# Spreading one-off loads over the steps of a pipelined stage, and putting a small copy first at that stage's start

## The chip, the cores and the metric

The kernel runs on one core of a Trainium2 chip. The metric is the device time of one execution, in microseconds (us), lower is better. The runs of one kernel in the same rounds lay within 0.15% (after, 4 runs) in one case and 1.4% (before, the 11 runs beside `start_only`) in another, and the same unaltered kernel gave medians between 1366 and 1376 us on the chips used here, so only runs of the same rounds on the same chip are compared with each other.

## The reference

The computation is the forward pass of a Branchformer-like block (attention in one branch, a gated depthwise convolution in the other, a depthwise merge convolution with K = 5 taps) and all its gradients. B = 2 sequences of T = 4000 tokens, D = 144 channels, bfloat16.

```python
# cut to what the change touches
m  = jnp.concatenate([glob, loc], axis=-1)            # two branches, 288 channels
mp = jnp.pad(m, ((0, 0), (pad, pad), (0, 0)))
mc = jnp.zeros_like(m)
for i in range(K):                                    # merge convolution, 5 taps
    mc = mc + mp[:, i:i + T, :] * dw_merge[i][None, None, :]
m = m + mc
return x + jnp.einsum('btc,cd->btd', m, w_merge)
# reference(): this and jax.vjp of it with grad_out -> out, dx, and 7 weight gradients
```

The gradients of the merge need the sum over all tokens of (output gradient, shifted by each tap) times (branch output). The kernel calls this the correlation and accumulates it in `EF`.

## The kernel before: the parts that matter

Each sequence goes through a head, an attention stage and a tail. The tail (`phase_tail`) runs in half steps h of two 128-token blocks each; a group g is four blocks, so h = 2g and 2g+1 belong to group g. For each group it

- loads `gs` (the output gradient with its five taps, 720 KB), `ug` (144 KB), `dh` (288 KB) and x (144 KB), the first three about two groups ahead, x at the group's start;
- correlates (`corr`) on TensorE. Its matmuls take 128 of the 144 channels, so the last 16 channels of each of the five taps are gathered into a narrow tile `g80` by GpSimd;
- writes 16 transposed rows to DRAM five times, each shifted by a tap (`taps.store`), and reads them back as 80 rows (`fill`), because the output convolution (`out_mm`) uses them as one operand `r80` a few half steps later.

```python
def prep(g):                                           # GpSimd, for group g
    r = slice(g * 4, g * 4 + 4)
    nc.gpsimd.memset(t3[:, r, 48:128], 0.0)
    nc.gpsimd.tensor_scalar(t3[:, r, 0:32], dh[:, r, 256:2 * D], 1.0, 0.0, ...)
    nc.gpsimd.tensor_scalar(t3[:, r, 32:48], S.Zn[:, r, 128:D], 1.0, 0.0, ...)
    g80 = G["g80", g] = lx.tile([128, 4, 80], BF, tag="g80", name="g80")
    nc.gpsimd.tensor_scalar(g80[:]..., G["gs", g][:, :, :, 128:D], 1.0, 0.0, ...)

# ... the main loop of the tail
loads(0); load_x(0); loads(1); prep(0)
for h in range(NPR + 4):                               # NPR = 16
    g, hf = divmod(h, 2)
    if hf == 0 and 0 < g < NGR:
        load_x(g)
    if 0 < h < NPR:
        turn_dx2(*turn_dx(h))                          # transposes of dh, Zn, t3
    if hf == 0 and g < NGR:
        turn(g, 0); corr(g, 0)                         # turn() ends with taps.store
        turn(g, 1); corr(g, 1)
    elif g < NGR:
        corr(g, 2)
        corr(g, 3)
    if h == 0:
        turn_dx2(*turn_dx(0))
    # ...
    if hf == 1 and 0 <= g - 1 < NGR:
        fill(g - 1)                                    # the two r80 loads
    # ...
    if h in (4, 6) and fin_:                           # second sequence only
        (fin_.loads if h == 4 else fin_.out_dwc)()
    # ...
    if 0 <= h - 4 < NPR:
        out_mm(h - 4)                                  # uses r80
    # ...
    if hf == 1 and g + 2 < NGR:
        loads(g + 2)                                   # gs, ug, dh
```

Every one of these transfers is issued by SyncE, in program order. An issue that must wait for something (an `r80` load must wait until the stores it reads from have landed; up to 4.5 us in the second tail of the kernel before) holds up all issues behind it.

`fin_.loads` exists only in the second sequence's tail. It fetches, in one piece of 11 issues at h = 4, what the final merge gradients need: the first sequence's `EF` sum in float32 (0.8 MB), its `gr` sum (288 KB) and eight weight tiles (0.8 MB together, one of them a few KB).

```python
def loads(self):
    for name, (dr, shp) in W.fin.items():              # WoT UT0 UT1 U0 U1 WmT Wqkv
        F[name] = fp.tile(shp, BF, name="f_" + name)
        nc.sync.dma_start(F[name][:], dr[:])
    # ...
    nc.sync.dma_start(self.EF0[:, 0:10, :], A.EF_d[:, 0:10, :])
    nc.sync.dma_start(self.EF0[0:80, 10:12, :], A.EF_d[0:80, 10:12, :])
    nc.sync.dma_start(self.gr0[:], A.gr_d[:])
    nc.sync.dma_start(self.Wk32[32:48, :], self.k.w_qkv[128:D, D:2 * D])
    # ... memsets
```

## Time and profile before

| | before |
|---|---|
| time, median of 3 runs | 1366.36 us (1363.06 to 1368.82) |
| profiled execution | span 1377.2 us, mean granted TensorE clock 0.977 |
| first tail, second tail: first to last correlation matmul | 72.6 us, 78.6 us |
| first use of r80 in half step 4 to that in half step 15, first and second tail | 51.2 us, 57.1 us |

The last two rows are worked out from matmul start times in the trace. I call them the *correlation stretch* and the *steady stretch*. The steady stretch leaves out the tail's start and its end; TensorE alone needs about 9.0 us for two half steps in it (in the first tail of before it is busy 49.5 of the 51.2 us of these 11 half steps).

The head of the profile's page (span, busy time of each engine, shares of the chain of work that ended last), kernel before:

```profile
span 1377.2 us, 40121 instructions
...
PE 1255.9 (91%) x15366; PEld 980.7 (71%) x15366; DVE 934.5 (68%) x3185; ACT 802.0 (58%) x2362; POOL 516.7 (38%) x919
...
PE 63%; DVE 12%; issue 8%; DMA 6%; ACT 5%; POOL 4%; SPq 1%; ACTq 0%; POOLq 0%; DVEq 0%
```

TensorE (PE) is busy 91% of the span and is 63% of the chain, so a wait of TensorE that goes away can be worth its length, and more where the granted clock was lower after it (0.50 after both waits shown below).

The waits of TensorE over the second tail and the end of the program, kernel before. The columns are what waited, what it waited for, the sum in us, how often, and the longest:

```profile
PE po L1992 <- DMA r<-y: 4.3, 1, 4.3
PE EF L1967 <- POOL g L1940: 3.0, 1, 3.0
PE pt L1977 <- POOL t3r L1938: 1.2, 1, 1.2
```

Two waits stand out. The first matters at the tail's start: the correlation waits 3.0 us for `g80`. The GpSimd timeline there (start, duration, line, operation, and in brackets the idle time before it with its cause) shows why:

```profile
1255.71 0.37 POOL L1936 MEMSET t3r<- 128x320 bf16 x1
1258.44 0.30 POOL L1937 TENSOR_SCALAR t3r<-dhr 128x128 bf16<-128x128 bf16 x1 [2.36 <-DMA dhr<-dh_d]
1258.71 0.24 POOL L1938 TENSOR_SCALAR t3r<-B_t 128x64 bf16<-128x64 bf16 x1
1258.91 0.46 POOL L1940 TENSOR_SCALAR g<-gs 128x320 bf16<-128x320 bf16 x1
```

The copy into `g80` (L1940) needs only `gs`, which is there, but it stands third in line behind a copy that waits 2.36 us for the DMA of `dh`. After the wait the microsecond windows show TensorE at clock 0.50 for 3.4 us, from about 1259.5 to 1262.9. The first tail shows the same (a wait of 3.05 us, then clock 0.50 from about 597.3 to 600.7).

The other wait, 4.3 us for `r80` (`r<-y`), lies in half step 6. The timeline of SyncE's DMA issues just before it, kernel before:

```profile
1277.62 0.45 SPq L1469 DMA_DIRECT2D y<-r  x1
1278.17 0.49 SPq L1469 DMA_DIRECT2D u<-r  x1
1278.71 0.42 SPq L2140 DMA_DIRECT2D f_WoT<-wf_WoT  x1
...
1284.00 0.43 SPq L2143 DMA_DIRECT2D f_EF<-EF_d  x1
...
1285.89 0.42 SPq L1472 DMA_DIRECT2D r<-y  x1
```

The 11 issues of `fin_.loads` begin at 1278.71 and end at 1285.85; the `r80` load stands behind all of them. One-microsecond windows of the same place (busy share and count for PE, weight loads, DVE, ACT, POOL, then the granted clock, the share of the DMA engines that was busy, GB/s):

```profile
1287.00:1288.00 1.00, 0.00 (x0) 0.00 (x0) 0.89 (x5) 0.02 (x1) 0.34 (x1) 1.00 0.95 348
...
1290.00:1291.00 1.00, 0.00 (x0) 0.00 (x0) 0.00 (x0) 0.00 (x0) 0.00 (x0) 0.60 1.20 216
1291.00:1292.00 1.00, 0.85 (x8) 0.85 (x9) 0.00 (x0) 0.00 (x0) 0.00 (x0) 0.50 1.04 321
...
1296.00:1297.00 1.00, 1.00 (x11) 1.00 (x9) 0.00 (x0) 0.97 (x4) 0.55 (x2) 0.50 0.00 0
```

TensorE stands still from 1286.8 to 1291.15, and after that runs at clock 0.50 until about 1297.

### The profile page before, as it was taken

The page shows a single profiled execution, that of the slowest core. Times are in us where ns is not written, and L with a number is a line of the kernel's source. Part 1 is how long each engine was busy: PE and PEld are TensorE (multiplying, and loading weights), DVE is VectorE, ACT ScalarE, POOL GpSimd, SP SyncE. Part 2 cuts the span into 40 slices and gives each one's busy share as a digit, 9 for nine tenths or more (in the row PEclk, how much of TensorE's full clock was granted, in tenths as well). Part 3 has the DMA queues.
Part 4 walks back from the last instruction along what each step waited for, and adds up shares of the span by engine and source line. Part 5 has one row for each costly group of instructions (what it writes and reads, how often), then busy time and mean ns, then how long its engine had stood idle before and what let it go on. Part 6 is the DMA issues. An engine that isn't in the chain of part 4 may idle for free.

```text
span 1377.2 us, 40121 instructions
## 1 busy us (share of the span) xinstructions
PE 1255.9 (91%) x15366; PEld 980.7 (71%) x15366; DVE 934.5 (68%) x3185; ACT 802.0 (58%) x2362; POOL 516.7 (38%) x919
## 2 busy tenths in 40 slices
PE   5799999999999998989878999999999999998896
PEld 2657777777776776789755777777776677668884
DVE  5466788688776785746454777877777677773564
ACT  3766666666666564444276666666665666543442
POOL 2212344444343342345340243444444344323550
PEclk9999999999999999999988999999999999999998
DMA  4459999999998989857563999999898889996761
GB/s 131 132 99 161 172 170 167 156 182 170 165 150 157 179 164 168 165 158 197 154 191 71 168 157 174 174 156 178 146 179 159 142 171 155 193 171 153 220 156 28
DMA packets 649706, 218.17 MB, mean 158 GB/s; under 512 B 587648, under 2 KB 646944, under 8 KB 649504
## 3 DMA queue, kind: packets, MB, share of 16 engines
q1 hardware_dynamic: 648448, 215.39, 80.7%
q8 instruction: 122, 2.00, 0.6%
q14 instruction: 80, 0.66, 0.1%
q10 hardware_dynamic: 1056, 0.13, 0.1%
HBM read 56.77 MB, written 23.89 MB: 59 GB/s over the span
## 4 chain that ended last, share of the span: by engine, by line
PE 63%; DVE 12%; issue 8%; DMA 6%; ACT 5%; POOL 4%; SPq 1%; ACTq 0%; POOLq 0%; DVEq 0%
PE y L1825 15%; PE pS L1786 8%; PE X L1845 7%; PE X L1846 7%; PE pD L1786 6%; PE pS L1782 4%; DVE Sm L1792 3%; PE pc L1518 2%; ACT Pm L1791 2%; DMA gnC<-gnC_d 2%; PE pb L1432 2%; PE po L1991 2%; PE EF L1967 1%; PE gr L2062 1%; POOL cc L2031 1%
## 5 line engine op out<-in xcount | busy, mean ns | idle before, releaser
L1792 DVE SCALAR_TENSOR_TENSOR Sm<-pD,Pm 128x500 bf16<-128x500 f32 x512 | 326.2, 674 | 210.2 <-ACT Pm L1791 191.5
L1791 ACT ACTIVATE Pm<-pS 128x500 bf16<-128x500 f32 x512 | 295.7, 585 | 91.2 <-PE pS L1786 87.2
L1845 PE MATMUL X<-Qs,Sm 128*128 128x144 bf16 x2048 | 292.9, 227 | 5.0 <-DVE acc L1858 5.0
L1846 PE MATMUL X<-Bt,Pm 128*128 128x144 bf16 x2048 | 293.0, 227 | 0.0
L1856 POOL TENSOR_TENSOR acc<-xs,acc 128x432 f32<-128x432 f32 x150 | 167.1, 1114 | 229.0 <-ACT xs L1855 228.6
L1846 PEld LDWEIGHTS <-Pm 128*128 128x128 bf16 x2048 | 201.0, 98 | 16.1 <-issue 5.8
L1845 PEld LDWEIGHTS <-Sm 128*128 128x128 bf16 x2048 | 201.1, 98 | 10.4 <-issue 0.3
L1855 ACT COPY xs<-X 128x432 f32<-128x432 f32 x150 | 77.7, 518 | 161.1 <-PE X L1846 156.8
L1825 PE MATMUL y<-xaa,PT 128*128 128x144 bf16 x2048 | 149.4, 226 | 8.7 <-DVE B_t L1833 8.4
L1786 PE MATMUL pS<-xaT,QTm 128*128 128x500 bf16 x512 | 154.3, 383 | 0.0
L1786 PE MATMUL pD<-xaT,BTm 128*128 128x500 bf16 x512 | 151.5, 377 | 0.0
L1825 PE MATMUL y<-xaa,ST 128*128 128x144 bf16 x2048 | 149.2, 226 | 0.0
L1825 PEld LDWEIGHTS <-PT 128*128 128x128 bf16 x2048 | 134.4, 98 | 18.9 <-issue 12.6
L1825 PEld LDWEIGHTS <-ST 128*128 128x128 bf16 x2048 | 133.9, 98 | 9.9 <-issue 0.5
L1814 POOL TENSOR_SCALAR nr<-nd,rl 128x1 f32<-128x1 f32 x64 | 22.0, 344 | 286.9 <-DVE nd L1808 263.0
L1858 DVE TENSOR_TENSOR acc<-X,acc 128x432 f32<-128x432 f32 x180 | 103.6, 576 | 27.3 <-PE X L1846 26.9
L1782 PE MATMUL pD<-XR,QBr 16*128 16x500 bf16 x512 | 109.7, 381 | 6.4 <-DVE Sm L1792 5.8
L1782 PE MATMUL pS<-XR,QBr 16*128 16x500 bf16 x512 | 103.6, 382 | 2.0 <-ACT QBr L1769 1.4
L1791 ACT ACTIVATION_READ_ACCUMULATOR Pm<-pS 128x1 f32 x512 | 103.6, 202 | 0.0
L1786 PEld LDWEIGHTS <-BTm 128*128 128x128 bf16 x512 | 50.4, 98 | 59.6 <-issue 1.7
L1786 PEld LDWEIGHTS <-QTm 128*128 128x128 bf16 x512 | 29.0, 97 | 72.1 <-issue 72.1
L1982 ACT COPY hT<-pt 128x1024 bf16<-128x1024 bf16 x32 | 32.4, 1012 | 66.3 <-PE pt L1977 66.3
(590 smaller groups left out, 2598.2 us busy)
## 6 DMA issues: line engine op xcount, KB each, us to landing
gs<-in_grad_out_dram SPq DMA_DIRECT2D x24, 720.0 KB
gtap<-gn_d SPq DMA_DIRECT2D x16, 720.0 KB
dh_d<-dh SPq DMA_DIRECT2D x32, 144.0 KB
dhr<-dh_d SPq DMA_DIRECT2D x16, 288.0 KB
gs<-in_grad_out_dram SPq DMA_DIRECT2D x8, 540.0 KB
xg<-in_x_dram SPq DMA_DIRECT2D x28, 144.0 KB
dug_d<-dug SPq DMA_DIRECT2D x16, 144.0 KB
gn_d<-gn_t SPq DMA_DIRECT2D x32, 72.0 KB
```

The source lines that it names most:

```text
L1432: nc.tensor.matmul(pb[:], goT[:, i * 128 + m:i * 128 + m + 128], W.GL[:, m, :, :].rearrange("p a b -> p (a b)"), start=(m == 0), stop=False)
L1782: nc.tensor.matmul(o_[:, 0:SC], QBr[rr, bi, :], S.XR[rr, c2, 0:SC], start=True, stop=False)
L1786: nc.tensor.matmul(p_[h][:, 0:SC], w_[:, bi, :], S.xaT[:, c0 + h * SC:c0 + (h + 1) * SC], start=False, stop=True)
L1791: nc.scalar.activation(P[:, pb, c1:c1 + SC], pS[h][:, 0:SC], ACT.Exp, accum_out=ld8[:, 0, n:n + 1])
L1792: nc.vector.scalar_tensor_tensor(Sm[:, pb, c1:c1 + SC], pD[h][:, 0:SC], 1.0, P[:, pb, c1:c1 + SC], op0=ALU.mult, op1=ALU.mult, accum_out=l ...
L1825: nc.tensor.matmul(y[:, w, :], src[:, jj, :], S.xaa[:, j, :], start=(j == 0), stop=(j == NBK - 1))
L1845: nc.tensor.matmul(X[:, jj, :], Sm[:, i % NP, j * 128:(j + 1) * 128], Qs[:, i % 4, :], start=(kk == 0 and jj == 0), stop=False, skip_group ...
L1846: nc.tensor.matmul(X[:, jj, :], P[:, i % NP, j * 128:(j + 1) * 128], Bt[:, i % 4, :], start=False, stop=(kk == 1), skip_group_check=True)
L1855: nc.scalar.copy(xs[:, 0:nj, :], X[:, 0:nj, :])
L1856: nc.gpsimd.tensor_tensor(a_, xs[:, 0:nj, :], a_, op=ALU.add)
L1858: nc.vector.tensor_tensor(a_, X[:, 0:nj, :], a_, op=ALU.add)
L1982: nc.scalar.copy(hT[:], pt[:])
```

## The change

The intent is to take away both waits. At the tail's start `g80` of group 0 is built first, the `dh` copy moves to the end of `prep`, and block 2's correlation moves behind the first transposes, so that half step 0 correlates three blocks. In the second tail the merge-gradient loads are cut into pieces, one per half step from h = 5 to h = 12, and the small dwc output moves from h = 6 to h = 14.

```diff
         def prep(g):
             r = slice(g * 4, g * 4 + 4)
+            def rows80():
+                g80 = ...; nc.gpsimd.tensor_scalar(g80..., G["gs", g][:, :, :, 128:D], ...)
+            if g == 0:
+                rows80()
             nc.gpsimd.memset(t3[:, r, 48:128], 0.0)
+            nc.gpsimd.tensor_scalar(t3[:, r, 32:48], S.Zn[:, r, 128:D], ...)
             nc.gpsimd.tensor_scalar(t3[:, r, 0:32], dh[:, r, 256:2 * D], ...)
-            nc.gpsimd.tensor_scalar(t3[:, r, 32:48], S.Zn[:, r, 128:D], ...)
-            g80 = ...; nc.gpsimd.tensor_scalar(g80..., G["gs", g][:, :, :, 128:D], ...)
+            if g:
+                rows80()
 ...
                 elif g < NGR:
-                    corr(g, 2)
+                    if g:
+                        corr(g, 2)
                     corr(g, 3)
                 if h == 0:
                     turn_dx2(*turn_dx(0))
+                    corr(0, 2)
 ...
-                if h in (4, 6) and fin_:
-                    (fin_.loads if h == 4 else fin_.out_dwc)()
+                if fin_ and 4 <= h < NPR - 1:
+                    fin_.loads(h - 4)
 ...
-    def loads(self):
+    def loads(self, n):
+        if n == 0:
+            ...                                        # tiles and memsets, no load
+        elif n < 5:                                    # h = 5, 6, 7, 8
+            q = slice(3 * n - 3, 3 * n)
+            if n < 4:                                  # 216 KB each
+                nc.sync.dma_start(self.EF0[:, q, :], A.EF_d[:, q, :])
+            else:                                      # 72 KB and 90 KB
+                nc.sync.dma_start(self.EF0[:, 9:10, :], A.EF_d[:, 9:10, :])
+                nc.sync.dma_start(self.EF0[0:80, 10:12, :], A.EF_d[0:80, 10:12, :])
+        elif n == 5:                                   # h = 9
+            nc.sync.dma_start(self.gr0[:], A.gr_d[:])
+        elif n == 6:
+            ...                                        # WmT, UT0, UT1
+        elif n == 7:
+            ...                                        # U0, U1, WoT
+        elif n == 8:
+            ...                                        # Wqkv, Wk32
+        elif n == 10:
+            ...                                        # the dwc output
```

More of the change, by code (lines that the diff above doesn't have):

```diff
@@ L1935, in prep @@
             r = slice(g * 4, g * 4 + 4)
+            def rows80():
+                g80 = G["g80", g] = lx.tile([128, 4, 80], BF, tag="g80", name="g80")
+                nc.gpsimd.tensor_scalar(g80[:].rearrange("p a (m r) -> p a m r", r=DR), G["gs", g][:, :, :, 128:D], 1.0, 0.0, op0=ALU.mult, op1=ALU.add)
+            if g == 0:
+                rows80()
             nc.gpsimd.memset(t3[:, r, 48:128], 0.0)
+            nc.gpsimd.tensor_scalar(t3[:, r, 32:48], S.Zn[:, r, 128:D], 1.0, 0.0, op0=ALU.mult, op1=ALU.add)
             nc.gpsimd.tensor_scalar(t3[:, r, 0:32], dh[:, r, 256:2 * D], 1.0, 0.0, op0=ALU.mult, op1=ALU.add)
-            nc.gpsimd.tensor_scalar(t3[:, r, 32:48], S.Zn[:, r, 128:D], 1.0, 0.0, op0=ALU.mult, op1=ALU.add)
-            g80 = G["g80", g] = lx.tile([128, 4, 80], BF, tag="g80", name="g80")
-            nc.gpsimd.tensor_scalar(g80[:].rearrange("p a (m r) -> p a m r", r=DR), G["gs", g][:, :, :, 128:D], 1.0, 0.0, op0=ALU.mult, op1=ALU.add)
+            if g:
+                rows80()
         def turn(g, h):
@@ L2133, in __init__ @@
         self.ps_t, self.ps_e, self.n = ps_t, ps_e, 0
-    def loads(self):
+    def loads(self, n):
         nc, A, W, fp = self.nc, self.k.A, self.W, self.fp
-        F = {}
-        for name, (dr, shp) in W.fin.items():
-            F[name] = fp.tile(shp, BF, name="f_" + name)
-            nc.sync.dma_start(F[name][:], dr[:])
-        self.WoT, self.UT, self.U, self.WmT, self.Wqkv = F["WoT"], [F["UT0"], F["UT1"]], [F["U0"], F["U1"]], F["WmT"], F["Wqkv"]
-        self.EF0 = fp.tile([128, 12, D], F32, name="f_EF0")
-        nc.sync.dma_start(self.EF0[:, 0:10, :], A.EF_d[:, 0:10, :])
-        nc.sync.dma_start(self.EF0[0:80, 10:12, :], A.EF_d[0:80, 10:12, :])
-        self.gr0 = fp.tile([128, 4, D], F32, name="f_gr0")
-        nc.sync.dma_start(self.gr0[:], A.gr_d[:])
-        self.Wk32 = fp.tile([128, D], BF, name="f_Wk32")
-        nc.gpsimd.memset(self.Wk32[:], 0.0)
-        nc.sync.dma_start(self.Wk32[32:48, :], self.k.w_qkv[128:D, D:2 * D])
-        self.ETr = fp.tile([128, 2, 5, D], BF, name="f_ETr")
-        nc.gpsimd.memset(self.ETr[:], 0.0)
-        self.Ej = [fp.tile([128, 2, 5, D], BF, name="f_Ej%d" % h) for h in range(2)]
-        for h in range(2):
-            nc.gpsimd.memset(self.Ej[h][:, 1, :, :], 0.0)
-        self.dU = fp.tile([128, 2, 2, D], F32, name="f_dU")
-        nc.gpsimd.memset(self.dU[:, :, 1, :], 0.0)
-        self.dwm = fp.tile([128, 2, 2, 5], F32, name="f_dwm")
-        nc.gpsimd.memset(self.dwm[:], 0.0)
-        self.dwcb = fp.tile([128, 2, 5], BF, name="f_dwcb")
-        nc.vector.tensor_copy(self.dwcb[:], A.dwc[:])
@@ L2162, in out_dwc @@
-    def out_dwc(self):
-        nc = self.nc
-        pt = self.T()
-        nc.tensor.transpose(pt[0:10, 0:128], self.dwcb[:].rearrange("p a b -> p (a b)"), self.W.ident[:])
-        o = self.fp.tile([16, 128], BF, name="f_dwct")
-        nc.scalar.copy(o[0:10, :], pt[0:10, 0:128])
-        nc.sync.dma_start(self.k.out5[:, 0:128], o[0:5, :])
-        nc.sync.dma_start(self.k.out5[:, 128:D], o[5:10, 112:128])
+        if n == 0:
+            self.F = {name: fp.tile(shp, BF, name="f_" + name) for name, (dr, shp) in W.fin.items()}
+            self.WoT, self.UT, self.U, self.WmT, self.Wqkv = self.F["WoT"], [self.F["UT0"], self.F["UT1"]], [self.F["U0"], self.F["U1"]], self.F["WmT"], self.F["Wqkv"]
+            self.dwcb = fp.tile([128, 2, 5], BF, name="f_dwcb")
+            nc.vector.tensor_copy(self.dwcb[:], A.dwc[:])
+            self.EF0 = fp.tile([128, 12, D], F32, name="f_EF0")
+            self.gr0 = fp.tile([128, 4, D], F32, name="f_gr0")
+            self.Wk32 = fp.tile([128, D], BF, name="f_Wk32")
+            nc.gpsimd.memset(self.Wk32[:], 0.0)
+            self.ETr = fp.tile([128, 2, 5, D], BF, name="f_ETr")
+            nc.gpsimd.memset(self.ETr[:], 0.0)
+            self.Ej = [fp.tile([128, 2, 5, D], BF, name="f_Ej%d" % h) for h in range(2)]
+            for h in range(2):
+                nc.gpsimd.memset(self.Ej[h][:, 1, :, :], 0.0)
+            self.dU = fp.tile([128, 2, 2, D], F32, name="f_dU")
+            nc.gpsimd.memset(self.dU[:, :, 1, :], 0.0)
+            self.dwm = fp.tile([128, 2, 2, 5], F32, name="f_dwm")
+            nc.gpsimd.memset(self.dwm[:], 0.0)
+        elif n < 5:
[8 more added lines that the diff above has]
+        elif n == 6:
+            for name in ("WmT", "UT0", "UT1"):
+                nc.sync.dma_start(self.F[name][:], W.fin[name][0][:])
+        elif n == 7:
+            for name in ("U0", "U1", "WoT"):
+                nc.sync.dma_start(self.F[name][:], W.fin[name][0][:])
+        elif n == 8:
+            nc.sync.dma_start(self.Wqkv[:], W.fin["Wqkv"][0][:])
+            nc.sync.dma_start(self.Wk32[32:48, :], self.k.w_qkv[128:D, D:2 * D])
+        elif n == 10:
+            pt = self.T()
+            nc.tensor.transpose(pt[0:10, 0:128], self.dwcb[:].rearrange("p a b -> p (a b)"), W.ident[:])
+            o = fp.tile([16, 128], BF, name="f_dwct")
+            nc.scalar.copy(o[0:10, :], pt[0:10, 0:128])
+            nc.sync.dma_start(self.k.out5[:, 0:128], o[0:5, :])
+            nc.sync.dma_start(self.k.out5[:, 128:D], o[5:10, 112:128])
```

## The prediction

> **What bounds it now.** The page of the kernel before has TensorE busy 91% of 1377.2 us; the chain of waits is 63% TensorE. The change touches only the two "tail" stages, 594 to 682 us and 1255 to 1377 us, and aims at three TensorE waits listed there:
>
> - In each tail the correlation (EF) waits for the narrow gradient columns g80: 3.05 us at 597.51, 3.01 us at 1259.42. In the GpSimd timeline the g80 copy (0.46 us) stands behind a copy of dh that itself waits 2.4 us for its DMA.
> - In the second tail the output convolution waits 4.3 us (1286.8 to 1291.15) for r80. In the DMA-issue timeline 11 merge-gradient loads (1278.71 to 1285.85) stand ahead of the r80 load.
>
> Each wait also halves the clock: by microsecond windows it is 0.5 from about 1259.3 to 1262.6 (same at 597) and from 1290.4 to 1297.0. [...]
>
> **What changes.** The same matmuls, copies, memsets and bytes; three more DMA issues (0.43 us each). Moved: g80 of group 0 goes first on GpSimd; block 2's correlation goes behind the first hT transposes; 1.9 MB of loads spread over eight half steps; the dwc output from half step 6 to 14.
>
> **Tail starts.** g80 should be ready near 594.3, when TensorE wants it: the 3.05 us wait goes, and about 1.7 us of half clock. Not all 4.7 us is kept: the first transposes now wait for dh(0) (landing 596.5), those of half step 2 for dh(1), which GpSimd sees at 602.0 in either version; before, they run at 605.1. I expect 2.8 us per tail, 5.6 us together, carried through because what follows is in series.
>
> **Second tail.** The r80 wait (4.3 us) and half of 5.9 us at half clock (2.9 us) go: 7.2 us. But the steady state has little slack: in the first tail, without these loads, the stretch from the first r80 use of half step 4 to that of 15 takes 51.2 us; in the second 57.1 us. So 5.9 us is the realistic ceiling. r80 loads are issued only 1.5 to 2.5 us before use there, since the queue sits up to 4.5 us until the preceding store lands. Each piece (216 to 288 KB, 0.6 to 0.8 us at the 350 GB/s seen when busy; an estimate) goes into that queue, half of them directly before an r80 load. I take 1.5 us back: 4.4 us net.
>
> **Total.** 5.6 + 4.4 = 10.0 us of 1366.4, 0.7%: 1356.4 us. Range 1350.5 to 1361.5. Chances: faster by over 2% 0.02, within 2% 0.97, slower 0.01.
>
> **Right if:** no TensorE wait on g80 over 0.5 us; clock 1.0 through both tail starts; about 1 us waits on dh in half steps 0 and 2 instead; half step 2 about 2.8 us sooner after the tail's start; in the second tail no r80 wait over 1 us at half step 6, but several of some tenths; half step 4 to 15 in 52 to 54 us; attention and heads unchanged.
>
> **Wrong if:** dh(1) lands later because group-2 loads start about 3.7 us sooner (gain under 2 us per tail); pieces delay r80 by over 1 us in each group (second gain near zero); short waits still halve the clock; or dh(1) lands sooner and the pieces fit into idle DMA time (up to 13 us).

The 1.7 us of half clock per tail start and the 5.9 us at half clock in the second tail are read from the windows of before.

## The result

| | before | after |
|---|---|---|
| median of 4 runs each, same rounds | 1366.38 us (1363.06 to 1368.82) | 1363.74 us (1362.58 to 1364.68) |
| ratio, 95% interval | | 0.9982 [0.9959, 1.0005] |
| profiled span, clock | 1377.2 us, 0.977 | 1360.7 us, 0.986 |
| correlation stretch, first tail, second tail | 72.6, 78.6 us | 69.6, 75.2 us |
| steady stretch, first tail, second tail | 51.2, 57.1 us | 51.1, 56.9 us |

A ratio here is the mean time of one kernel's runs over the mean of the other's runs of the same rounds, so it is not quite the ratio of the medians that are quoted. The change is within noise or a gain of a few us: 2.6 us by these medians, where 10.0 were predicted. The time lies above the predicted range.

The two profiled executions differ by 16.5 us, far more than the timed runs do. Of that, 7.0 us lies in the first attention stage (526.1 us before, 519.1 after), ahead of every changed instruction of that sequence, and 1.6 us in the second one. A profile is one execution; over all 20 profiles the first attention stage takes 519 to 527 us, whatever the kernel. The two tails together account for 6.5 us of the 16.5.

The head of the page, kernel after:

```profile
span 1360.7 us, 40124 instructions
...
PE 1246.5 (92%) x15366; PEld 973.8 (72%) x15366; DVE 933.6 (69%) x3185; ACT 801.8 (59%) x2362; POOL 515.8 (38%) x919
...
PE 65%; DVE 12%; DMA 9%; issue 6%; ACT 5%; POOL 2%; SPq 1%; ACTq 0%; DVEq 0%; POOLq 0%
```

TensorE's waits over the second tail and the end, kernel after:

```profile
PE pt L1983 <- DMA dhr<-dh_d: 5.5, 6, 2.2
...
PE pt L1983 <- POOL t3r L1944: 1.1, 1, 1.1
...
PE po L1998 <- DMA r<-y: 0.5, 1, 0.5
```

There is no wait for `g` (that is `g80`) left, and only 0.5 us for `r<-y`. In their place come six waits for the DMA of `dh` (`dhr<-dh_d`), 5.5 us together, which before were not in the list. The GpSimd timeline at the tail's start, kernel after:

```profile
1242.60 0.46 POOL L1939 TENSOR_SCALAR g<-gs 128x320 bf16<-128x320 bf16 x1
1243.00 0.36 POOL L1942 MEMSET t3r<- 128x320 bf16 x1
1243.33 0.24 POOL L1943 TENSOR_SCALAR t3r<-B_t 128x64 bf16<-128x64 bf16 x1
1245.42 0.30 POOL L1944 TENSOR_SCALAR t3r<-dhr 128x128 bf16<-128x128 bf16 x1 [1.84 <-DMA dhr<-dh_d]
```

The start works as intended: `g80` comes first, and the copy that waits for `dh` stands last.

Where the second tail loses what it gained is seen from when each half step's first `r80` matmul starts, in us after the tail's start:

| half step | 4 | 6 | 8 | 9 | 10 | 12 | 14 | 15 |
|---|---|---|---|---|---|---|---|---|
| before | 21.9 | 35.5 | 47.2 | 51.2 | 56.1 | 65.1 | 74.1 | 79.0 |
| after | 18.7 | 27.6 | 37.5 | 41.5 | 50.3 | 60.3 | 71.6 | 75.6 |

At half step 8 the kernel after is 9.7 us ahead; at half step 15 it is 3.4 us ahead, which is about what the start alone had given it (3.2 at half step 4). The largest single loss is at half step 10, in the timeline of TensorE, kernel after:

```profile
1288.06 0.40 PE L1983 MATMUL pt<-w_ident,dhr 128*128 128x128 bf16 x2 [2.24 <-DMA dhr<-dh_d]
```

TensorE waited 2.24 us for `dh` of group 5. The timeline of SyncE's issues before it, kernel after:

```profile
1278.63 0.42 SPq L2166 DMA_DIRECT2D f_EF<-EF_d  x1
...
1280.19 0.59 SPq L1112 DMA_DIRECT2D gs<-in_grad_out_dram  x1
...
1281.42 0.42 SPq L1931 DMA_DIRECT2D dhr<-dh_d  x1
...
1282.41 0.94 SPq L1469 DMA_DIRECT2D y<-r  x1
1283.48 0.90 SPq L1469 DMA_DIRECT2D u<-r  x1
1284.42 0.47 SPq L2168 DMA_DIRECT2D f_EF<-EF_d  x1
1284.93 0.68 SPq L2169 DMA_DIRECT2D f_EF<-EF_d  x1
1289.09 0.32 SPq L1472 DMA_DIRECT2D r<-y  x1
```

This is one turn of the queue's cycle. A piece of `EF` (L2166, 216 KB, half step 7) goes ahead of the loads of group 5. The `dh` load is issued at 1281.42 and has landed only when TensorE goes on at 1288.06. The two tap stores take 0.94 and 0.90 us just to be issued (0.45 and 0.49 in the timeline of before), and the next `r80` load waits until 1289.09, 6.7 us after the issue of its store. The windows around it, kernel after:

```profile
1286.00:1287.00 1.00, 0.00 (x0) 0.00 (x0) 0.31 (x1) 0.00 (x0) 0.00 (x0) 1.00 0.99 284
1287.00:1288.00 1.00, 0.00 (x0) 0.00 (x0) 0.00 (x0) 0.00 (x0) 0.00 (x0) 0.94 0.32 97
1288.00:1289.00 1.00, 0.94 (x9) 0.80 (x10) 0.00 (x0) 0.00 (x0) 0.91 (x3) 0.50 0.15 51
...
1290.00:1291.00 1.00, 1.00 (x12) 1.00 (x9) 0.28 (x1) 0.69 (x2) 0.58 (x1) 0.50 0.95 125
```

After this wait of 2.24 us the granted clock is 0.50 from about 1287.9 to 1291.3. The waits inside the steady half steps (0.29, 2.24, 0.69 and 1.14 us for `dh`, 0.5 us for `r80`) add to 4.9 us; a stretch without any piece (`noload`, 50.8 us, below) has 1.1 us of such waits. The difference of 3.8 us, with about 1.7 us for the half clock (an estimate: half of the 3.4 us at clock 0.50 in these windows), accounts for 5.5 of the 6 us that separate the two.

### The profile page after: what moved, and what is told of

It reads as the page before. It is cut to its first block, busy times and chain, and to the rows that moved or that the text cites. A ratio compares the mean times of both kernels' runs of the same rounds, so it can differ in the third digit from the quotient of the medians.

```text
span 1360.7 us, 40124 instructions
## 1 busy us (share of the span) xinstructions
PE 1246.5 (92%) x15366; PEld 973.8 (72%) x15366; DVE 933.6 (69%) x3185; ACT 801.8 (59%) x2362; POOL 515.8 (38%) x919
## 4 chain that ended last, share of the span: by engine, by line
PE 65%; DVE 12%; DMA 9%; issue 6%; ACT 5%; POOL 2%; SPq 1%; ACTq 0%; DVEq 0%; POOLq 0%
PE y L1825 15%; PE pS L1786 8%; PE X L1845 7%; PE X L1846 7%; PE pD L1786 6%; PE pS L1782 4%; DVE Sm L1792 4%; PE pc L1518 2%; DMA dhr<-dh_d 2%; DMA gnC<-gnC_d 2%; PE pb L1432 2%; PE po L1997 2%; ACT Pm L1791 2%; PE EF L1973 2%; PE gr L2068 1%
## 5 line engine op out<-in xcount | busy, mean ns | idle before, releaser
L1786 PEld LDWEIGHTS <-BTm 128*128 128x128 bf16 x512 | 50.2, 98 | 59.3 <-issue 1.1
```

Source lines behind the costliest of these rows:

```text
L1786: nc.tensor.matmul(p_[h][:, 0:SC], w_[:, bi, :], S.xaT[:, c0 + h * SC:c0 + (h + 1) * SC], start=False, stop=True)
```

## The experiments

The theory after reading the result: the start of the tail gives what was predicted or more, and the pieces cost the second tail what the removal of the long `r80` wait had gained, because the steady cycle of the one issue queue has no slack. Its rivals: the start gives less than predicted; the cost is that of more issues rather than of bytes; the cost comes because the tap stores land late behind the pieces; or the pair of profiles differs by chance.

Every kernel with a ratio in this section ran five rounds. The stretches are read from one profile per run. Between repeats of one kernel the steady stretch differs by up to 1.5 us in the second tail (2.1 in the first), the correlation stretch by up to 2.5 us.

### Halves of the change: start_only and loads_only

`start_only` is before with the new `prep` and the new order of `corr`; `loads_only` is after without them.

```diff
 # start_only, against the kernel after          # loads_only, against the kernel after
-    if fin_ and 4 <= h < NPR - 1:               -    if g == 0: rows80()
-        fin_.loads(h - 4)                       -    ... dh copy last
+    if h in (4, 6) and fin_:                    +    ... prep in the order of before
+        (fin_.loads if h == 4                   -    if g: corr(g, 2) ... corr(0, 2)
+         else fin_.out_dwc)()                   +    corr(g, 2)
```

> Only the tail-start part of the change (g80 first, third block behind the transposes); the merge loads stay in one piece at half step 4. Theory A (the start part works fully and is kept, the second part gains nothing): first tail's correlation stretch 69.6 us (73 before), second tail's start 3.2 us sooner at half step 4, then the r80 wait of about 4 us with half clock at half step 6 as before, half step 4 to 15 57 us; correlation stretch of the second tail 75.3 us; in total 6.3 us faster than before, the same as the whole change. Rival B (the new start makes the second tail's DMA burst denser, and only spreading saves it): the r80 wait at half step 6 grows to over 6 us and the second tail gains under 1 us.

> Only the spreading of the merge loads and the later dwc output; tail starts as before. Theory A: no r80 wait at half step 6, but waits for dh of 0.5 to 2.5 us in later even half steps; half step 4 to 15 stays at 56 to 58 us, so the time is that of before within 1 us. Rival B: without the earlier start the pieces find idle DMA time, half step 4 to 15 falls to 52 to 54 us, 4 us faster than before.

| | ratio to before, 95% | corr. stretch, tail 1, tail 2 | steady stretch, tail 2 |
|---|---|---|---|
| start_only (1366.06 against 1375.86) | 0.9943 [0.9899, 0.9986] | 70.1, 74.8 us | 56.3 us |
| loads_only (1374.16 against 1375.86) | 1.0002 [0.9960, 1.0044] | 73.0, 81.9 us | 58.2 us |

The loads part alone gave nothing: removing the 4.3 us wait left the steady stretch of the second tail no shorter. The start part alone was at least as good as the whole change; it kept the `r80` wait at half step 6 (4.0 us, where rival B asked for over 6). `loads_only` leaves the first tail as before, and `start_only` shortens it by 2.5 us in this pair of profiles.

### Is it the pieces? late and tiny

`late` keeps the four `EF` pieces at h = 5 to 8 but moves all the others (gr0 and the weights, 1.1 MB) behind the steady half steps. `tiny` moves the same and keeps every issue at h = 5 to 12, but shrinks each to one partition: the issues stay, the bytes go. The sum then uses other data in place of `EF0` (relative error 0.706). Its output is wrong, which doesn't matter for the time.

```diff
 # late
-    if fin_ and 4 <= h < NPR - 1:
+    if fin_ and 4 <= h < NPR + 2:
-        elif n in (5, 6, 7, 8): ...             # gr0, WmT UT, U WoT, Wqkv
+        elif n == 10: ... WmT, UT0, UT1 too
+        elif n == 12: ... U0, U1, WoT
+        elif n == 13: ... Wqkv, Wk32, gr0
 # tiny, on top of that
-    nc.sync.dma_start(self.EF0[:, q, :], A.EF_d[:, q, :])
+    nc.sync.dma_start(self.EF0[0:1, q, :], A.EF_d[0:1, q, :])   # and so for each piece, n = 1 to 8
```

> The whole change, but the merge loads that are not needed before half step 16 (gr, and all seven weight matrices, together 0.9 MB) move from half steps 9 to 12 to half steps 14, 16 and 17; the EF pieces (0.8 MB) stay at half steps 5 to 8. Theory A (each piece lengthens the cycle store, landing, r80 load, next group's loads by its bytes): the dh wait of about 2.2 us at half step 10 stays, those at 12 and 14 fall under 0.5 us; half step 4 to 15 about 54 us, total 2 to 3 us faster than the whole change. Rival C (without its stall the second tail runs into DMA latency whatever is loaded): 56 to 57 us, no gain. Rival D: the late loads delay the end, and the time from the last correlation to the end grows by over 1 us.

> Wrong result on purpose: every DMA issue of the spread merge loads stays where the change puts it, but moves one partition's row instead of 128 (the correlation sum then takes another array in place of the first sequence's part; the weights and gr load whole at half steps 14 to 17). Theory A (bytes): the dh waits of half steps 8 to 14 nearly vanish, half step 4 to 15 51 to 52 us as in the first tail, which has none of these loads; 5 us faster than the whole change. Rival E (the time of the issues on the one queue, 0.4 us each, 13 of them): half step 4 to 15 stays over 55 us.

| | ratio to before, 95% | corr. stretch, tail 1, tail 2 | steady stretch, tail 2 |
|---|---|---|---|
| late (1367.36 against 1375.86) | 0.9946 [0.9905, 0.9987] | 70.4, 75.3 us | 53.0 us |
| tiny (1365.94 against 1375.86) | 0.9944 [0.9900, 0.9988] | 69.8, 71.5 us | 53.4 us |

Both shorten the steady stretch by more than 3 us against the 56.9 us of after. That `late` took 53.0 us speaks against its rival C (56 to 57 us whatever is loaded). `late` did not shorten the second correlation stretch in its profile, because its tail lost about 4 us at the start: `dh` of group 1 landed late (GpSimd saw it 10.5 us after the tail's start, where most profiles have 7.6 to 8.5), and a 2.8 us wait followed, and after it clock 0.50 for 3.4 us (from about 1261.3 to 1264.7). This lies before any of the moved loads. By time the two are not told apart from `start_only`.

### The same kernel again, more bytes, and another queue: after_again, double, actstore, late_act

`after_again` is after, unaltered. `double` adds bytes in the same places (216 KB in seven half steps, 72 KB in h = 7), with five more issues. `actstore` issues the tap stores of the tail from ScalarE, so that they do not stand in SyncE's queue behind the pieces. `late_act` is `late` with the same stores.

```diff
 # double (more bytes in the same half steps)
-            q = slice(3 * n - 3, 3 * n)
+            q = slice(3 * n - 3, min(3 * n + 3, 10))
+            # and one more load of 216 KB of EF0 at n = 4 to 8
 # actstore
-    def store(self, src, t0, w):
+    def store(self, src, t0, w, eng=None):
-        self.nc.sync.dma_start(dst, ...)
+        (eng or self.nc.sync).dma_start(dst, ...)
-            taps[h].store(r_[112:128, :], g * 512, 512)
+            taps[h].store(r_[112:128, :], g * 512, 512, nc.scalar)
```

> The changed kernel unaltered, once more, on the chip and in the rounds of the other runs: the two tails as in its first profile (correlation stretches 69.6 and 75.2 us, half step 4 to 15 of the second tail 56 to 58 us). Theory A (the start part is all that is kept, and the first comparison of 0.9982 was small because the untouched attention stages scatter by several us from run to run): ratio to before 0.993 to 0.997, as start_only had. Rival G (the change slows the attention stages): ratio over 0.997 again and attention stages 3 us longer than those of the other kernels of this call.

> The change with more bytes in the same half steps: EF pieces are loaded a second time (over the same values, 216 KB more in each of eight half steps, 5 more issues); the result stays right. Theory A (bytes): each cycle from one group's loads to the next grows by about 1.2 us (2 times 216 KB at 350 GB/s), half step 4 to 15 of the second tail 60 to 63 us, 4 to 5 us slower than after_again. Rival E (issue time alone, 5 times 0.4 us): at most 59 us.

> The change, but the stores of the narrow transposed rows (y, u) that the r80 loads wait for are issued by ScalarE instead of by the one queue behind the group's loads. Theory H (the pace is set by the serial chain store, landing, r80 load, next group's loads on one queue, and the store waits there in line): the store lands within 4 us of its issue instead of 6.6, the cycle falls from 11.3 us to under 10, half step 4 to 15 of the second tail 52 to 54 us, 3 us faster than after_again. Rival I (the store waits for the same DMA engines whoever issues it): landing still over 6 us, 56 to 58 us.

> late and actstore together: fewer bytes in the second tail's cycle and the stores out of line. Theory H with A: half step 4 to 15 51 to 52 us, 5 us faster than after_again, near 0.990 of before. Rival I: as late, 53 to 54 us.

All four against a median of 1370.81 us. The last column is, here and below, the mean over the second tail's three turns from group 4 to group 7; in the first tails it is 9.2 to 9.5 us in most profiles:

| | median | ratio to before, 95% | steady stretch, tail 2 | mean time from one gs load to the next |
|---|---|---|---|---|
| after_again | 1368.80 us | 0.9986 [0.9967, 1.0005] | 58.1 us | 12.2 us |
| double | 1370.06 us | 1.0011 [0.9984, 1.0037] | 61.0 us | 12.7 us |
| actstore | 1369.77 us | 0.9999 [0.9976, 1.0021] | 54.1 us | 10.2 us |
| late_act | 1366.17 us | 0.9978 [0.9956, 1.0000] | 50.9 us | 9.5 us |

The repeat of after did not meet its expectation of 0.993 to 0.997; whether the attention stages grew (rival G) is open: its second one is the longest of all profiles, 528.9 us, but in `after_third` below the two stages are no longer than in `start_only_2` of the same rounds (1049.0 and 1050.6 us together). `double`'s more bytes in the same places made the steady stretch longer, by 3 to 4 us; five issues more should cost under 1 us of that (an estimate from the about 2 us of 14 bare issues below), so bytes count. In `actstore` the text's theory H asked that the stores land within 4 us, and that failed: from the issue of a store to the `r80` load that waits for it took 5.1 to 6.5 us in groups 2 to 5 of the second tail, about as in after (5.3 to 6.7 us); its rival I was right that the landing would not come sooner, while the reason it gives (the same DMA engines) was not shown by any run. The queue's cycle still fell, from about 12 to 10.2 us, which the freed issue time of SyncE (1.84 us for the two stores in the cycle shown above) can explain. But the start of the tail then lost about 2 us: half step 4 came at 20.4 to 21.1 us instead of 18.8, since ScalarE waited about 0.5 us for the copy that feeds each store and 0.31 us for each issue. The time of `actstore` shows no gain, and `late_act`, expected near 0.990, came to 0.9978.

### A null test, two repeats and a better version: before_again, start_only_2, after_third, late_act2

`late_act2` is `late_act`, with the stores of the first two groups left on SyncE, to spare the tail's start.

```diff
-            taps[h].store(r_[112:128, :], g * 512, 512)
+            taps[h].store(r_[112:128, :], g * 512, 512, nc.scalar if g > 1 else nc.sync)
```

> The kernel before, timed against itself: ratio 1.000 within about 0.003, which shows how far chance alone moves a ratio; and a second profile of it: correlation stretches of its tails 72 to 73 us and 78 to 80 us, half step 4 to 15 of the second tail 57 to 58 us. Theory A (first profile typical in the tails): both as in the first profile. Rival J (the first profile, of a run 13 us slower than the median, had a slow second tail too, and the change's gain there is overstated): second tail under 77 us.

> The tail-start part alone, again, now in the same rounds as the whole change. Theory A: faster than before by 3 to 6 us (ratio 0.995 to 0.998), and no slower than the whole change, because spreading the loads gains nothing on top of it. Rival K (the spread does help and the first ratio of 0.9943 was chance): the whole change is faster than this by 3 us or more.

> The whole change a third time. Theory A: ratio 0.995 to 0.9985, second tail's half step 4 to 15 at 56 to 58 us with dh waits in even half steps 8 to 14, first tail's correlation stretch 69 to 70 us. Rival K: half step 4 to 15 under 55 us.

> late_act with the stores of the first two groups back on the one queue, so that the tail start (which late_act delayed by 1.6 us, ScalarE waiting for the copy that it stores) is that of the change. Theory H with A: half step 4 reached 18.7 us after the tail's start, half step 4 to 15 at 49 to 51 us in both tails; 8 to 10 us faster than before and 5 us faster than the whole change (ratio to before 0.992 to 0.994). If the start gain and the later gain trade against each other (rival L: the loads and stores of the later groups then collide again), no faster than late_act.

All against a median of 1372.13 us:

| | median | ratio to before, 95% | corr. stretch, tail 1, tail 2 | steady stretch, tail 2 |
|---|---|---|---|---|
| before_again | 1373.51 us | 1.0011 [0.9984, 1.0037] | 75.0, 76.5 us | 56.5 us |
| start_only_2 | 1370.05 us | 0.9976 [0.9949, 1.0002] | 69.8, 73.3 us | 54.8 us |
| after_third | 1370.82 us | 0.9962 [0.9929, 0.9996] | 70.8, 76.6 us | 57.9 us |
| late_act2 | 1361.31 us | 0.9915 [0.9887, 0.9943] | 68.1, 74.4 us | 52.9 us |

The null test says how far to trust a ratio: the same kernel against itself gave 1.0011. Its profile also met the mark of rival J (76.5 us, under 77): the first pair of profiles overstated the gain in the second tail, so means over repeats are used below. The three comparisons of after with before gave 0.9982, 0.9986 and 0.9962, a mean of 0.9977 or about 3 us. Against `start_only` (0.9943 and 0.9976) the whole change is not better, and their intervals overlap. `start_only`, `late`, `tiny` and `after_third` have intervals below 1 too, but the repeats of the first and the last reach 1.0002 and 1.0005; `late_act2` lies furthest below. Its profile does not explain that: half step 4 of its second tail came at 21.9 us and not at the 18.7 expected (`dh` of group 1 was late, 9.7 us), its steady stretch was 52.9 us and not 49 to 51, and `late_act` had the shorter tails.

### The place within the cycle: noload, tiny_2, odd, even

An issue in an even half step comes right behind the tap stores and just ahead of the `r80` load; one in an odd half step comes right behind the `r80` loads and ahead of the next group's `gs`, `ug` and `dh`. The change does both. `odd` and `even` issue exactly the same pieces, two per odd or two per even half step. `noload` is `tiny` without the eight sets of issues at all (wrong too); `tiny_2` repeats `tiny`.

```diff
+        # odd:  {1: (1, 2), 3: (3, 4), 5: (5, 6), 7: (7, 8)}     h = 5, 7, 9, 11
+        # even: {2: (1, 2), 4: (3, 4), 6: (5, 6), 8: (7, 8)}     h = 6, 8, 10, 12
+        for m in {0: (0,), 10: (10,), ...}.get(n, ()):
+            self.piece(m)                                         # the loads(n) of the change
```

> Wrong result on purpose: the change without any merge load before half step 14 (the correlation sum takes another array in place of the first sequence's part; weights and gr load at half steps 14 to 17). If the loads are all that separates the second tail from the first, half step 4 to 15 is 51 to 52 us, as in first tails. If tiny's 53.4 us was not the time of its issues but something else in the second tail, it is 53 to 54 us here too.

> tiny once more, for a second profile. Bytes as the main cause: 52 to 54 us again. Issues as the main cause: 55 us or more.

> The change with the same pieces, bytes and issues, but two pieces at a time and only in odd half steps, right behind an r80 load and ahead of the next group's loads. Theory A (bytes count wherever they stand in the cycle): half step 4 to 15 56 to 59 us, as the change has (56.9 to 58.1). Theory M (only pieces just behind the stores hurt, because the r80 load waits for those): 53 to 55 us.

> The same pieces, two at a time, only in even half steps, right behind the stores and ahead of the r80 load. Theory A: 56 to 59 us. Theory M: 59 to 61 us, with r80 waits. Theory N (behind the stores they use the time in which the queue waits and the DMA engines run dry, and hurt least): 53 to 55 us.

| (one run each; state unknown) | corr. stretch, tail 2 | steady stretch, tail 1, tail 2 | mean time from one gs load to the next |
|---|---|---|---|
| noload | 70.1 us | 51.5, 50.8 us | 9.6 us |
| tiny_2 | 71.0 us | 50.2, 52.5 us | 10.5 us |
| odd | 77.9 us | 50.5, 59.2 us | 12.5 us |
| even | 69.0 us | 53.2, 51.1 us | 9.7 us |

This gives the sizes, to 1 or 2 us. Without any piece the steady stretch is 50.8 us (one profile; the first tails, which have no pieces either, take 51.4 on average with the stores on SyncE), so the pieces of the change cost 57.6 (the mean of three profiles of after) minus 50.8, or 6.8 us. The bare issues cost about 2 us (52.5 and 53.4). The same bytes cost nothing measurable when all stand in even half steps, and 8.4 us when all stand in odd ones. That is not twice the cost of the change, which has only half of them there; no run has the odd half of the change alone, so how its 6.8 us divide between its odd and even pieces is not shown.

### Odd and even, timed: odd_2 and even_2

> odd timed and profiled a second time, in the same rounds. Theory N: half step 4 to 15 57 to 60 us, correlation stretch of the second tail 76 to 79 us, 6 to 9 us slower than even_2, ratio 0.997 to 1.001. If the place does not matter: equal to even_2.

> even timed and profiled a second time. Theory N (pieces right behind the stores are free; pieces ahead of a group's loads delay the loads, with them the next stores and r80 loads): half step 4 to 15 of the second tail 50 to 53 us, correlation stretch of the second tail 69 to 71 us; with the first tail's 3.6 us this is 10 to 12 us faster than before, ratio 0.990 to 0.994. If the first profile was luck: 55 us or more, ratio 0.996 or more.

Same kernels as above, five rounds against a median of 1371.11 us:

| | median | ratio to before, 95% | corr. stretch, tail 2 | steady stretch, tail 2 |
|---|---|---|---|---|
| odd_2 | 1371.56 us | 1.0001 [0.9969, 1.0033] | 78.0 us | 59.3 us |
| even_2 | 1363.25 us | 0.9949 [0.9919, 0.9979] | 71.5 us | 50.7 us |

The medians lie 8.3 us apart, as the steady stretches do (8.6 us). The two kernels differ only in which half step each piece is issued. `odd_2` met its expectation; `even_2`, 7.9 us faster than before, fell short of the 10 to 12 expected, and its second tail reached half step 4 only at 21.2 us, since `dh` of group 1 was late there too (9.6 us). TensorE's waits over the second tail and the end, first `even_2`:

```profile
PE pt L1983 <- DMA dhr<-dh_d: 2.9, 3, 1.9
...
PE po L1998 <- DMA r<-y: 1.1, 1, 1.1
```

and `odd_2`:

```profile
PE pt L1983 <- DMA dhr<-dh_d: 7.3, 6, 2.0
PE po L1998 <- DMA r<-u: 1.4, 2, 0.9
```

In `even_2` the longest wait for `dh`, 1.9 us, lies at the tail's start, before any piece. One turn of the issue queue in `even_2`:

```profile
1284.75 0.50 SPq L1112 DMA_DIRECT2D gs<-in_grad_out_dram  x1
...
1286.87 0.45 SPq L1469 DMA_DIRECT2D y<-r  x1
...
1287.83 0.43 SPq L2170 DMA_DIRECT2D f_EF<-EF_d  x1
1288.31 0.48 SPq L2172 DMA_DIRECT2D f_EF<-EF_d  x1
1289.80 0.33 SPq L2173 DMA_DIRECT2D f_EF<-EF_d  x1
1292.84 0.33 SPq L1472 DMA_DIRECT2D r<-y  x1
```

and in `odd_2`:

```profile
1285.46 0.42 SPq L2170 DMA_DIRECT2D f_EF<-EF_d  x1
...
1287.97 0.55 SPq L1112 DMA_DIRECT2D gs<-in_grad_out_dram  x1
1288.62 2.00 SPq L1930 DMA_DIRECT2D ug<-ug_d  x1
...
1291.68 0.43 SPq L1469 DMA_DIRECT2D y<-r  x1
...
1296.24 0.32 SPq L1472 DMA_DIRECT2D r<-y  x1
```

From one `gs` issue to the store, to the `r80` load, to the next `gs` issue, `even_2` takes 2.1, 6.0 and 1.9 us, 10.0 in all; `odd_2` 3.7, 4.6 and 3.8 us, 12.1 in all; and after, in the cycle shown above, 2.2, 6.7 and 2.4 us, 11.3 in all. In `even_2` the three pieces are issued between 1287.83 and 1290.13, in time that SyncE would have spent waiting for its store to land, and the wait is hardly longer than in `noload` (5.8 us there for the same group). In `odd_2` they stand in front of the `gs` load, and behind them a single issue (L1930) takes 2.00 us. So the timelines read as if the pieces push out the loads of the next group and all that follows in the serial cycle.

## Why the prediction was wrong, point by point

**What bounds the kernel, and the three waits: right.** The 3.0 us waits for `g80` and the 4.3 us wait for `r80` were there, had the causes named, and all three went away.

**Tail starts: right, a little under-sized.** There is no `g80` wait, the clock is 1.0 in the starts of both tails of after, and short waits of about 1 us take its place (0.76, 0.38 and 1.08 us in the second tail). The full clock is not sure with the new start: in `late` and `even_2`, where `dh` of group 1 came late (10.5 and 9.6 us after the tail's start), a wait of 2.8 and 1.9 us in half step 2 of the second tail was followed by 3.4 us at clock 0.50. Half step 4 of the second tail came 3.2 us sooner in the pair of profiles. Over all profiles, the first tail's correlation stretch is 69.9 us in 14 profiles with the new start (stores on SyncE) and 73.5 us in the three without, so 3.7 us and not 2.8. In the second tail, before to `start_only` is 77.6 to 74.1 us (two profiles each), 3.5 us. That makes 7.2 where the sum had 5.6.

**The ceiling of the second tail: right.** The prediction put it at 5.9 us. The steady stretch is 56.8 us in the two profiles of before and 50.8 without any piece: 6.0 us.

**The step that failed: "I take 1.5 us back: 4.4 us net."** The pieces, placed as the change places them, cost 6.8 us and not 1.5, so the net was not 4.4 us gained but 0.8 us lost (57.6 against 56.8). The prediction had reckoned each piece by its transfer time, 0.6 to 0.8 us, and took back 1.5 us for all eight, without saying where the rest goes. It had named this as a way to be wrong ("pieces delay r80 by over 1 us in each group (second gain near zero)"), and the outcome, no gain, was that one, though by another wait: TensorE waited mostly for `dh`, and for `r80` 0.9 us at most in the three profiles of after.

**The reason beside that step was also wrong in its sign.** "Half of them directly before an r80 load" names the half that is harmless when all pieces stand there (`even`). Pieces right before an `r80` load went into the time in which the queue waits for the store to land (4.5 us by the prediction's own reading; in `even`, `even_2` and `noload` 4.8 to 6.0 us from the store's issue to the `r80` load in groups 2 to 5), and the steady stretch stayed at 51 us. Ahead of the next group's loads they do the damage: 59 us when all were placed there. Accordingly "no r80 wait over 1 us at half step 6" came true, but "several of some tenths" did not in the profile of after, which has one of 0.5 us (`after_again` has three, 0.44 to 0.86 us); the longer waits were on `dh`, up to 2.24 us. The half steps 4 to 15 took 56.9 us and not "52 to 54".

**What is shown and what is argued.** It is shown that the place decides (even against odd, same bytes, same issues, same rounds; the odd pieces also stand one half step earlier throughout, which no run tests apart), that bytes cost more than the issues (`tiny`, `double`), and that moving the stores to another queue did not make them land sooner (5.1 to 6.5 us in `actstore`, 5.3 to 6.7 us in after). That each late group pushes the next one, because its store follows its loads in the same queue and the next `r80` load waits for that store, is what the timelines look like, but no run isolates it. Why 0.65 us of transfer (an estimate: 216 KB at 331 GB/s, the window 1288:1289 of before) grows to some 1.7 us for each of the four odd half steps (if the even ones are free) stays open. The half clock has a part in after (the 1.7 us estimated above, of 6), and how large its part is in the repeats is not shown; and single long issues, where 0.45 us is usual, also occur in first tails, where no piece exists (1.40 us for a `gs` load in before).

**The sum.** Predicted were 5.6 + 4.4 = 10.0 us. In the tails of the profiles, 3.7 us came in the first and 1.4 us in the second (77.6 to 76.2), 5.1 together. The timed mean of three comparisons is about 3 us. The difference between the two is within the scatter of the attention stages.

**Better versions.** `even_2` (0.9949) and `late_act2` (0.9915) both beat before clearly. Which of them is the faster is open, since they ran in different rounds and their intervals overlap. `even` is the smaller step from the change: the same pieces, in even half steps only.

## What to carry to other kernels

Spreading a burst of background loads evenly is not by itself cheap: in a queue that issues in order, look for the place in its cycle where it stands waiting anyway (here, after the stores, ahead of the load that waits for them), and put the pieces there, not ahead of the loads that start the next turn (51 us against 59 us for the same pieces here). When you cost such pieces, measure how long the cycle takes against what the bounding engine needs (here, in the first tails, about 9.4 us of cycle against 9.0 us of TensorE); with that little slack the pieces of the change were not absorbed but cost 6.8 us. And before you read a 16 us difference from two profiles, check the stages that the change did not touch: here, each attention stage scattered by about 8 us.

## What else the traces show

- The length of TensorE's wait did not by itself tell whether the clock fell after it. It was 0.50 after 3.01 and 4.34 us (before), 2.24 us (after), 2.8 us (`late`) and 1.9 us (`even_2`). It stayed at 1.00 after about 2 us in `odd_2` (windows 1293 to 1301), 1.4 us in `noload` (1260 to 1263) and 1.14 us in after (1308 to 1312). What decides between the cases near 2 us is not shown.
- Moving issues to another engine left the landing as it was (5.1 to 6.5 us from ScalarE, 5.3 to 6.7 us from SyncE), and the usual 0.45 us of an issue is small against that. But single issues in these tails took up to 2.00 us in the timelines above (the `ug` load in `odd_2`), and with two issues per group moved to ScalarE the cycle took 10.2 us instead of about 12 (that the issue time alone did this is not shown).
- The place of background loads in the issue queue, relative to a load that must wait for a store, made 51 us against 59 us for the same loads.
- The landing of one and the same load scatters: `dh` of group 1, issued in the same place of the program, was seen by GpSimd between 7.6 and 10.5 us after the tail's start; the latest (`late`) cost about 4 us, for no cause that the traces show.
